# Twenty more split tiles of q and k, token numbers written once a batch, interleaved last products, five accumulators for x, and weights ahead of counts, in a kernel of attention over channels and a mixture of experts

## The chip, the cores and the metric

The kernel runs on one core of a Trainium2 chip. The time is that of the device, in microseconds (us), for one launch; of several runs the median counts. The engines are TensorE (PE in the profile, PEld its weight loads), VectorE (DVE), ScalarE (ACT), GpSimd (POOL) and SyncE (SP, which here only issues DMAs).

## The reference

```python
# q, k, v: (B=4, N=3648, C=256)
qn = q / (norm(q, axis=1) + 1e-6); kn = k / (norm(k, axis=1) + 1e-6)
s = kn.transpose(0, 2, 1) @ qn / tau          # (B, C, C): over channels
a = softmax(s, -1)
x = (v @ a).reshape(14592, 256)
# 16 experts: 4 groups of 4; each token goes to the best group's best expert
g_w = softmax(x @ w_group)[best group]
e_w = softmax(x @ w_expert[group])[best expert]
out[token] = g_w * e_w * (relu(x @ w1[g, e]) @ w2[g, e])      # 256 -> 1024 -> 256
```

All is fp32. Both softmaxes of the routing add 1e-9 to their sum.

## The kernel before

**Attention.** A batch has 3648 rows, that is 28 tiles of 128 and a rest of 64. They are read in units of 4 tiles (q and k together, 512 rows, tile `qkraw`); a batch has 8 units, the eighth is the rest. Unit `u` belongs to batch `u // 8`. `s_load` reads a unit, `s_split` prepares it, `s_mm` adds its products k^T q to the accumulator `sacc` in PSUM, `s_add` sums the squares for the norms. An fp32 product shows as two records on PE, so a plain tile is 4 records (two halves of k). In all units but the rests and two others the tile `SPLIT = 3` goes another way: ACT copies it rounded to fp32r (`qkhi`, L195), DVE subtracts that from the original (`qklo`, L196), and three fp32r products, hi·hi, hi·lo and lo·hi, take the place of the fp32 one: 6 records per tile. There are 26 such tiles. After a batch's last unit, `softmax` makes the matrix `a`, split into `ahi` and `alo` too (L292), with 20 routing columns beside the 256.

**x and the routing.** `x_tr` transposes v on PE (`vtr`), and splits it into `vth` (ACT, L313) and `vtl` (DVE, L314). `x_mm` makes each row tile of x and its 20 logits by six fp32r products of 276 columns into one of three PSUM accumulators (`xmm`, tag `mm`); ACT empties it into `xs` (L335), a ring of 10 tiles of 4 rows each. The 20 logits are copied to `L`, by DVE (L342), or by ACT (L340) when `x_mm` is called with hooks, as in the last batch. The generator `routing(b, j0, j1)` (L349 to L425) works on a range of row tiles, in nine calls (`RANGES`): first the one-hot of the best expert, its running count (`inc`, L387), then the slot numbers `si` (bs at L400 to si at L409), then the weights (sw at L412 to the reciprocal at L423, which goes straight into column 257 of `xs`). `scatter` (L430 to L455) sends one row tile to its slots in DRAM (`x_sorted`): POOL writes the token numbers into column 256 of `xs` (an iota per group of four tiles, L441, or L443 for the rest), issues the indirect DMA (L444), and fills a tile with zeros (L158) as a pause. SP fetches the first item's rows (L676) when batch 2's tiles below 20 have been scattered.

**Experts.** 28 items of 512 sorted rows: transposes (L747), first layer (L898), second layer (L918 wide, hi part; L919 narrow, low part), weighting and a send per 128 rows (indirect DMA on POOL, L947). The last item ends with four turns (L1233 to L1243): wide products (L1238) into the accumulator of 128 rows, ACT reads its one half with the weight (L1239), narrow products (L1241) into the other half, DVE adds it (L1242), send.

The order of SP and POOL is written by hand throughout. PE, ACT and DVE are ordered by a scheduler up to the 30th step of a loop over units, and by hand from there (`hooks`, lists of small steps between the row tiles of x).

Of the kernel before, what the change touches and what calls it, by code (L numbers as in the profile page):

```python
# [17 lines left out]
P = 128  # L18
# [6 lines left out]
NJ = J + 1  # L25
# [27 lines left out]
PLAIN = (GPB + 1, GPB + 2)  # L53
US = UX = B * GPB
XOFF = GPB + 2
VX = 1
# [4 lines left out]
def attention_moe(ctx: ExitStack, tc, q, k, v, tau, w_group, w_expert, w1, w2, out):  # L61
# [89 lines left out]
    for n in range(4):  # L151
        DVE.memset(lane4[n * PC:(n + 1) * PC, n:n + 1], 1.0)
    zero = cp.tile([P, RW], F32, name="zero")
# [32 lines left out]
    def s_split(u):  # L186
        b, g = divmod(u, GPB)
        rows, nj = rows_of(g)
        x, d = su[u], st[b]
        raw = x["raw"]  # L190
        x["split"] = SPLIT if g < NG and u not in PLAIN else None
        if x["split"] is not None:
            x["hi"] = spool.tile([P, 2, C], F32R, tag="hi", name="qkhi")
            x["lo"] = spool.tile([P, 2, C], F32R, tag="lo", name="qklo")
            ACT.activation(x["hi"], raw[:, :, SPLIT, :], AF.Copy)  # L195
            DVE.tensor_tensor(x["lo"], raw[:, :, SPLIT, :], x["hi"], ALU.subtract)  # L196
        if g == 0:
# [15 lines left out]
    def s_mm(u):  # L213
        b, g = divmod(u, GPB)
        rows, nj = rows_of(g)
        x, d = su[u], st[b]
        for j in range(nj):
            if j == x["split"]:
                hi, lo = x["hi"], x["lo"]
# [97 lines left out]
    def x_mm(u, hooks=None):  # L317
# [9 lines left out]
        for j in range(nj):  # L327
            mm = ps.tile([P, 512], F32, tag="mm", name="xmm", bufs=3)
# [10 lines left out]
        if hooks:  # L339
            ACT.activation(Lx, xs[:rows, :nj, C:NE], AF.Copy)  # L340
        else:
            DVE.tensor_copy(Lx, xs[:rows, :nj, C:NE])  # L342


    scatters, pend, now, rows_at, early = [], [], [0], {}, []
# [4 lines left out]
    def routing(b, j0=0, j1=NJ):  # L350
# [31 lines left out]
        if j1 == NJ:  # L382
            DVE.memset(oh[REM:, :, nj - 1:nj], 0.0)
        yield
# [7 lines left out]
        ez = wide("ez", NL)  # L392
        ACT.activation(ez, z, AF.Exp)
        pp = pt.tile([P, 512], F32, tag="misc", name="pp", bufs=1)
        with tc.high_priority(offset=0 if now[0] >= TM else -1040):
            PE.matmul(pp[:, 0:E], tri, rs, start=True, stop=False, skip_group_check=True)
            PE.matmul(pp[:, E:2 * E], onesb, rs, start=False, stop=True, skip_group_check=True)
        yield
# [11 lines left out]

        sw = wide("sw", 5).rearrange("p (j g) -> p j g", g=5)
        DVE.tensor_reduce(sw, ez.rearrange("p (j g e) -> p j g e", g=5, e=4), AX.X, ALU.add)  # L412
        yield
        sg = wide("sg", 4).rearrange("p (j g) -> p j g", g=4)
        DVE.tensor_tensor(sg, sw[:, :, 1:5], ohg, ALU.mult)
        se = wide("se", 1)
        DVE.tensor_reduce(se, sg, AX.X, ALU.add)
        DVE.tensor_scalar(se, se, 1e-9, None, ALU.add)
        DVE.scalar_tensor_tensor(se, sw[:, :, 0], 1e-9, se, ALU.add, ALU.mult)

        for g in range(j0 // GJ, -(-j1 // GJ)):
            n = min(GJ, j1 - g * GJ)
            DVE.reciprocal(rows_at[b, g][:, 0:n, C + 1], se[:, g * GJ - j0:g * GJ - j0 + n])  # L423
# [6 lines left out]
    def scatter(n, wait=0):  # L430
        for _ in range(n):
# [22 lines left out]
            pause()  # L454

# [718 lines left out]
    for n in range(len(seq) + lag):  # L1174
# [56 lines left out]
        if n == len(seq) + lag - 1:  # L1231
# [3 lines left out]
            for t in (0, 2, 1, 3):  # L1235
                tsl, a, wcol = slice(t * P, (t + 1) * P), d["acc"][t], d["wc"][:, t:t + 1]
                for f in range(8 - TAIL, 8):
                    PE.matmul(a, d["h", f][0][:, tsl], d["w2w"][:, :, f, :], start=False, stop=(f == 7), skip_group_check=True)  # L1238
                ACT.activation(d["ys"][:, t, :], a[:, 1, :], AF.Copy, scale=wcol)  # L1239
                for f in range(8 - TAIL, 8):  # L1240
                    PE.matmul(a[:, 0, :], d["h", f][1][:, tsl], d["w2h"][:, f, :], start=False, stop=(f == 7), skip_group_check=True)  # L1241
                DVE.scalar_tensor_tensor(d["ys"][:, t, :], a[:, 0, :], wcol, d["ys"][:, t, :], ALU.mult, ALU.add)  # L1242
# [94 lines left out]
```

## Time and profile before

| | us |
|---|---|
| median of 3 runs (lowest, highest) | 931.75 (929.29, 934.0) |
| profiled execution, its own time | 935.83 |
| profiled execution, span | 934.1 |
| PE, busy in the span | 916.0 |
| DVE, busy | 707.0 |
| ACT, busy | 481.4 |
| POOL, busy | 403.1 |

The span runs from the first instruction to the last. Busy times of different engines overlap. The chain that ended last follows the work back from the end, at each step to what released it. A line such as "L196 DVE" is an instruction's line in the kernel; "out<-in" are its tiles, and "xcount" how many instructions stand in the row.

### The profile page before, as it was taken

How to read it: one execution, taken by the hardware profiler on the slowest of the kernel's cores; microseconds unless marked ns; L12 is line 12 of the kernel's file. 1: busy time of each engine (PE TensorE's matmuls, PEld its weight loads, DVE VectorE, ACT ScalarE, POOL GpSimd, SP SyncE). 2: the span in 40 equal slices, each digit the busy share in tenths (PEclk: the TensorE clock that was granted, in tenths of full speed). 3: DMA queues.
4: the chain of work that ended last, by engine and by line, in shares of the span. 5: the costliest groups of instructions: out<-in, count | busy, mean ns of one | idle time of the engine just before them, and what ended most of it. 6: DMA issues, size and time to landing. Idle time of an engine off the chain costs nothing.

```text
span 934.1 us, 17126 instructions
## 1 busy us (share of the span) xinstructions
PE 916.0 (98%) x5620; PEld 771.7 (83%) x5620; DVE 707.0 (76%) x1478; ACT 481.4 (52%) x791; POOL 403.1 (43%) x573
## 2 busy tenths in 40 slices
PE   9999999998999999999999999999999999999996
PEld 7898998987899988888888887888888888888884
DVE  6888968766889877978775778678766877687742
ACT  6787677556654544444444444444444444444431
POOL 0001888986578682223222433343334333333222
PEclk9999999999999999999999999999999999999999
DMA  9974868355855577677777777777777767776740
GB/s 305 350 284 174 302 230 278 143 192 183 265 175 175 201 231 240 226 241 256 243 242 245 254 251 244 243 248 239 228 237 232 248 226 228 234 242 231 235 136 27
DMA packets 159172, 213.97 MB, mean 229 GB/s; under 512 B 63107, under 2 KB 117643, under 8 KB 159072
## 3 DMA queue, kind: packets, MB, share of 16 engines
q1 hardware_dynamic: 144128, 168.23, 55.2%
q0 software_dynamic: 14944, 44.54, 12.6%
q8 instruction: 46, 0.75, 0.3%
q14 instruction: 54, 0.44, 0.1%
HBM read 170.33 MB, written 31.39 MB: 216 GB/s over the span
## 4 chain that ended last, share of the span: by engine, by line
PE 73%; issue 9%; DMA 5%; POOL 5%; DVE 4%; ACT 3%; SPq 1%; POOLq 0%; ACTq 0%; DVEq 0%
PE hmm L898 28%; PE wacc L918 16%; PE wacc L919 8%; PE xmm L332 6%; PE yacc L927 5%; PE sacc L227 4%; DMA qkraw<-in_k 3%; POOL out L947 2%; PE qacc L1034 2%; PE qmm L1021 2%; PE vtr L312 2%; DVE sqa L211 2%; POOL x_sorted L444 1%; POOL zero L158 1%; DMA xg<-x_sorted,ix_big 1%
## 5 line engine op out<-in xcount | busy, mean ns | idle before, releaser
L898 PE MATMUL hmm<-xth,ww 128*128 128x512 f32 x896 | 316.1, 394 | 0.1
L907 ACT ACTIVATE hh<-hmm 128x512 fp32r<-128x512 f32 x222 | 133.6, 602 | 346.7 <-PE hmm L898 316.1
L947 POOL DMA_INDIRECT out<-ys,ids x112 | 133.8, 1195 | 385.0 <-DVE ys L936 355.4
L918 PE MATMUL wacc<-ww,hh 128*128 128x512 f32 x752 | 274.7, 398 | 0.0
L908 DVE SCALAR_TENSOR_TENSOR hl<-hmm,hh 128x512 fp32r<-128x512 f32 x222 | 153.0, 690 | 133.8 <-ACT hh L907 118.9
L919 PE MATMUL wacc<-ww,hl 128*128 128x256 f32 x752 | 210.8, 280 | 0.0
L898 PEld LDWEIGHTS hmm<-xth,ww 128*128 128x128 f32 x896 | 168.1, 188 | 38.1 <-ACT xth L748 0.4
L898 PE MATMUL hmm<-xtl,ww 128*128 128x512 f32 x448 | 177.3, 396 | 0.2 <-DVE xtl L749 0.2
L918 PEld LDWEIGHTS wacc<-ww,hh 128*128 128x128 f32 x752 | 141.3, 188 | 43.2 <-issue 7.8
L444 POOL DMA_INDIRECT x_sorted<-xs,si x112 | 133.5, 1192 | 65.0 <-issue 31.9
L919 PEld LDWEIGHTS wacc<-ww,hl 128*128 128x128 f32 x752 | 141.1, 188 | 6.9
L709 DVE TENSOR_TENSOR ww<-wraw,ww 128x1024 fp32r<-128x1024 f32 x112 | 136.8, 1221 | 13.1 <-ACT ww L708 12.0
L708 ACT ACTIVATE ww<-wraw 128x1024 fp32r<-128x1024 f32 x112 | 118.6, 1059 | 0.0
L898 PEld LDWEIGHTS hmm<-xtl,ww 128*128 128x128 f32 x448 | 84.5, 189 | 10.5 <-DVE xtl L749 0.5
L227 PE MATMUL sacc<-qkraw 128*128 128x256 f32 (+1 forms) x360 | 87.0, 385 | 1.2 <-DMA qkraw<-in_k 1.2
L158 POOL MEMSET zero<- 128x256 f32 x264 | 87.8, 333 | 0.3
L332 PE MATMUL xmm<-ahi,vth 128*128 128x276 f32 (+1 forms) x232 | 70.2, 305 | 4.9 <-ACT xs L335 3.8
L227 PEld LDWEIGHTS sacc<-qkraw 128*128 128x128 f32 (+1 forms) x360 | 65.5, 192 | 10.1 <-issue 2.2
L332 PE MATMUL xmm<-alo,vth 128*128 128x276 f32 (+1 forms) x232 | 67.6, 292 | 0.2 <-DVE alo L292 0.2
L332 PE MATMUL xmm<-ahi,vtl 128*128 128x276 f32 (+1 forms) x232 | 66.9, 289 | 0.0
L211 DVE TENSOR_TENSOR sqa<-sqa,sq 128x2048 f32<-128x2048 f32 (+1 forms) x28 | 57.6, 2056 | 10.4 <-ACT sq L203 10.0
L335 ACT ACTIVATE xs<-xmm 128x276 f32<-128x276 f32 x112 | 42.6, 405 | 37.3 <-PE xmm L332 23.2
(269 smaller groups left out, 1283.2 us busy)
## 6 DMA issues: line engine op xcount, KB each, us to landing
wraw<-in_moe_w SPq DMA_DIRECT2D x55, 1024.0 KB
wraw<-in_moe_w SPq DMA_DIRECT2D x50, 512.0 KB
qw<-in_moe_w SPq DMA_DIRECT2D x48, 512.0 KB
vr<-in_v SPq DMA_DIRECT2D x28, 512.0 KB
qkraw<-in_q SPq DMA_DIRECT2D x26, 512.0 KB
qkraw<-in_k SPq DMA_DIRECT2D x26, 512.0 KB
xq<-xg SPq DMA_DIRECT2D x368, 32.0 KB
x_sorted<-xs,si POOLq DMA_INDIRECT x112
```

What stands on the lines that cost most here:

```text
L158: POOL.memset(zero[:, 0:256], 0.0)
L227: PE.matmul(d["acc"][:, c, :], kt[:rows, 1, cs], qt[:rows, 0, :], start=d.pop("first", True) and c == 0, stop=(g == NG), skip_group_check= ...
L332: PE.matmul(mm[:rows, :NE], vt[:, c, j * P:j * P + rows], at[:, c, :], start=(n == 0), stop=(n == 5))
L444: ins = POOL.indirect_dma_start(out=xs_d, out_offset=bass.IndirectOffsetOnAxis(ap=si[:rows, j:j + 1], axis=0), in_=xs[:rows, t, 0:RW].bitc ...
L708: ACT.activation(whs[n][:, s], raw[:, s], AF.Copy)
L709: DVE.tensor_tensor(wls[n][:, s], raw[:, s], whs[n][:, s], ALU.subtract)
L898: PE.matmul(mm, wt[:, c, fs], xt[:, c, :], start=(n == 0), stop=(n == 5))
L907: ACT.activation(hh, mm, AF.Relu)
L908: d["hl"] = DVE.scalar_tensor_tensor(hl, mm, 0.0, hh, ALU.max, ALU.subtract)
L918: PE.matmul(d["acc"][t], hh[:, tsl], d["w2w"][:, :, f, :], start=(f == 0), stop=(f == 7), skip_group_check=True)
L919: PE.matmul(d["acc"][t][:, 0, :], hl[:, tsl], d["w2h"][:, f, :], start=False, stop=(f == 7), skip_group_check=True)
L947: ins = POOL.indirect_dma_start(out=out, out_offset=bass.IndirectOffsetOnAxis(ap=d["ids"][:, t:t + 1], axis=0), in_=d["ys"][:, t, :], in_o ...
```

## The change

1. `MORE` names 20 further tiles to be split: tile 2 in units 14 to 27 (12 of them, since the rests are left out), tiles 1 and 2 of unit 28, tiles 0, 1 and 2 of units 29 and 30. Their hi and lo parts use buffers `hh` and `hl`, which are the experts' later (3 of each).
2. The token numbers go to a tile `tok`, by two iotas for a batch (all 28 tiles, and the rest), those of the first two batches at the start, the others behind a batch's last scatter. The reciprocal goes to `tok` as well, once per routing call, and small DVE instructions (an OR with 0) copy number and weight into `xs`, one for each group of tiles.
3. The last products: wide 0, wide 2, narrow 0, wide 1, narrow 2, wide 3, narrow 1, narrow 3, with a send behind each narrow.
4. In the last batch two of five row tiles of x take an `acc` buffer as accumulator, beside the three `mm`.
5. In `routing` the exponential comes one step earlier, and weights and copies to `xs` stand ahead of the slot numbers; one step fewer.
6. The copy to `L` is always ACT's.

```diff
+MORE = {**{u: (2,) for u in range(GPB + 6, 28)}, 28: (1, 2), 29: (0, 1, 2), 30: (0, 1, 2)}
+NTOK = 2
...
+    tok = cp.tile([P, NTOK, NJ, 2], F32, name="tok")
+    def number(b):
+        o = tok[:, b % NTOK, :, 0].bitcast(I32)
+        POOL.iota(o[:, 0:J], pattern=[[-1, J]], base=NOID - b * NT, channel_multiplier=-J)
+        POOL.iota(o[:, J:NJ], pattern=[[0, 1]], base=NOID - b * NT - J * P, channel_multiplier=-1)
+    for b in range(NTOK):
+        number(b)
...
-        x["split"] = SPLIT if g < NG and u not in PLAIN else None
-        if x["split"] is not None:
-            x["hi"] = spool.tile([P, 2, C], F32R, tag="hi", name="qkhi")
-            x["lo"] = spool.tile([P, 2, C], F32R, tag="lo", name="qklo")
-            ACT.activation(x["hi"], raw[:, :, SPLIT, :], AF.Copy)
-            DVE.tensor_tensor(x["lo"], raw[:, :, SPLIT, :], x["hi"], ALU.subtract)
+        x["split"] = {}
+        for j in (*MORE.get(u, ()), SPLIT) if g < NG and u not in PLAIN else ():
+            if j == SPLIT:
+                hi, lo = [spool.tile([P, 2, C], F32R, tag=n, name="qk" + n) for n in ("hi", "lo")]
+            else:
+                hi, lo = [hp.tile([P, 512], F32R, tag=n, name=n).rearrange("p (i c) -> p i c", i=2) for n in ("hh", "hl")]
+            ACT.activation(hi, raw[:, :, j, :], AF.Copy)
+            DVE.tensor_tensor(lo, raw[:, :, j, :], hi, ALU.subtract)
+            x["split"][j] = hi, lo
...
-            mm = ps.tile([P, 512], F32, tag="mm", name="xmm", bufs=3)
+            spread.append(u)
+            if hooks and d is st[B - 1] and len(spread) % 5 < 2:
+                mm = ps.tile([P, 2, C], F32, tag="acc", name="xmm").rearrange("p c n -> p (c n)")
+            else:
+                mm = ps.tile([P, 512], F32, tag="mm", name="xmm", bufs=3)
...
-        if hooks:
-            ACT.activation(Lx, xs[:rows, :nj, C:NE], AF.Copy)
-        else:
-            DVE.tensor_copy(Lx, xs[:rows, :nj, C:NE])
+        ACT.activation(Lx, xs[:rows, :nj, C:NE], AF.Copy)
...
+        DVE.reciprocal(tok[:, b % NTOK, j0:j1, 1], se)
+        for g in range(j0 // GJ, -(-j1 // GJ)):
+            n = min(GJ, j1 - g * GJ)
+            DVE.tensor_single_scalar(rows_at[b, g][:, 0:n, C:C + 2].bitcast(I32),
+                                     tok[:, b % NTOK, g * GJ:g * GJ + n, :].bitcast(I32), 0, op=ALU.bitwise_or)
...
-        for g in range(j0 // GJ, -(-j1 // GJ)):
-            n = min(GJ, j1 - g * GJ)
-            DVE.reciprocal(rows_at[b, g][:, 0:n, C + 1], se[:, g * GJ - j0:g * GJ - j0 + n])
...
-            if t == 0:
-                tok = xs[:, 0:nj, C].bitcast(I32)
-                if g < NG:
-                    POOL.iota(tok, pattern=[[-1, GJ]], base=NOID - b * NT - g * GJ, channel_multiplier=-J)
-                else:
-                    POOL.iota(tok, pattern=[[0, 1]], base=NOID - b * NT - J * P, channel_multiplier=-1)
...
+            if j0 + j == NJ - 1 and b + NTOK < B:
+                number(b + NTOK)
...
+            turns = (0, 2, 1, 3)
+            wide_of(turns[0])
+            for t, nxt in zip(turns, (*turns[1:], None)):
+                if nxt is not None:
+                    wide_of(nxt)
+                narrow_of(t)
                 send(d, t)
```

The order of instructions shows three places. On PE, the last products of the last item, before the change; `wacc` with its number is the accumulator of 128 rows, `eh` and `hh` are hi parts of the hidden layer, `el` and `hl` low parts:

```order
L1238 MATMUL wacc_12239<-ww3_3702,eh_12297 128x512 x2
L1238 MATMUL wacc_12239<-ww3_3702,hh_12333 128x512
L1238 MATMUL wacc_12239<-ww3_3702,hh_12344 128x512
L1241 MATMUL wacc_12239<-ww3_3702,el_12298 128x256 x2
L1241 MATMUL wacc_12239<-ww3_3702,hl_12334 128x256
L1241 MATMUL wacc_12239<-ww3_3702,hl_12345 128x256
L1238 MATMUL wacc_12241<-ww3_3702,eh_12297 128x512 x2
```

And the same place after it, where the lines are L1248 (wide) and L1254 (narrow):

```order
L1248 MATMUL wacc_12385<-ww3_3879,eh_12443 128x512 x2
L1248 MATMUL wacc_12385<-ww3_3879,hh_12479 128x512
L1248 MATMUL wacc_12385<-ww3_3879,hh_12490 128x512
L1248 MATMUL wacc_12387<-ww3_3879,eh_12443 128x512 x2
L1248 MATMUL wacc_12387<-ww3_3879,hh_12479 128x512
L1248 MATMUL wacc_12387<-ww3_3879,hh_12490 128x512
L1254 MATMUL wacc_12385<-ww3_3879,el_12444 128x256 x2
L1254 MATMUL wacc_12385<-ww3_3879,hl_12480 128x256
L1254 MATMUL wacc_12385<-ww3_3879,hl_12491 128x256
L1248 MATMUL wacc_12386<-ww3_3879,eh_12443 128x512 x2
```

Between the wide and the narrow products of one accumulator now stand the wide ones of the next. On DVE, the routing call for tiles 8 to 20 of batch 2, before the change (`vtl` belongs to x, `inc` to `si` are the slot numbers, `sw` to the reciprocal the weights):

```order
L390 CAST rs<-inc 128x16
L288 COPY ax<-awp 128x2x20
L292 TENSOR_TENSOR alo<-ax,ahi 128x552
L314 TENSOR_TENSOR vtl<-vtr,vth 128x512 x2
L400 TENSOR_TENSOR bs<-pp,carry 128x16
...
L409 CAST si<-sf 128x12
L412 TENSOR_REDUCE sw<-ez 128x60
...
L423 RECIPROCAL xs<-se 128x4 x3
L314 TENSOR_TENSOR vtl<-vtr,vth 128x512 x2
```

And after it:

```order
L407 CAST rs<-inc 128x16
L302 COPY ax<-awp 128x2x20
L306 TENSOR_TENSOR alo<-ax,ahi 128x552
L328 TENSOR_TENSOR vtl<-vtr,vth 128x512 x2
L414 TENSOR_REDUCE m_2819<-ez 128x60
...
L421 RECIPROCAL tok<-se 128x12
L424 TENSOR_SCALAR xs<-tok 128x4x2 x3
L428 TENSOR_TENSOR bs<-pp,carry 128x16
...
L437 CAST si<-sf 128x12
```

The weights moved ahead of the slot numbers, and one reciprocal with three copies stands for three reciprocals. On POOL, the scatters of one group and the next before the change:

```order
L444 DMA x_sorted<-xs,si 238080x272
L158 MEMSET zero 128x256
L441 IOTA xs 128x4
L444 DMA x_sorted<-xs,si 238080x272
L158 MEMSET zero 128x256
```

And after it, at the end of a batch:

```order
L452 DMA x_sorted<-xst,si 238080x272
L169 MEMSET zero 128x256
L159 IOTA tok 128x28
L160 IOTA tok 128x1
L452 DMA x_sorted<-xs,si 238080x272
```

An iota stands no longer ahead of each group of four scatters; two stand behind a batch's last one (and four at the start of the program).

## Rows read from the trace of the kernel before

**Rows 1.** The page: busy time by engine, and the chain that ended last.

```profile
PE 916.0 (98%) x5620; PEld 771.7 (83%) x5620; DVE 707.0 (76%) x1478; ACT 481.4 (52%) x791; POOL 403.1 (43%) x573
...
PE 73%; issue 9%; DMA 5%; POOL 5%; DVE 4%; ACT 3%; SPq 1%; POOLq 0%; ACTq 0%; DVEq 0%
```

**Rows 2.** Windows: length, busy time of each engine (instructions), granted clock, DMA share, GB/s.

```profile
100.00:140.00 40.00, 39.58 (x274) 36.92 (x274) 32.54 (x76) 27.24 (x48) 35.95 (x48) 1.00 0.77 270
140.00:180.00 40.00, 39.46 (x271) 36.49 (x271) 35.60 (x86) 28.02 (x52) 34.60 (x47) 1.00 0.68 232
180.00:196.00 16.00, 16.00 (x108) 14.72 (x106) 9.33 (x26) 7.35 (x14) 14.11 (x25) 1.00 0.29 96
...
232.00:236.00 4.00, 3.63 (x30) 3.41 (x29) 3.11 (x8) 3.43 (x10) 0.00 (x0) 1.00 0.60 176
```

**Rows 3.** PE's timeline around 106 us: start, length, instruction, [idle before].

```profile
105.63 1.89 PE L227 MATMUL sacc<-qkraw 128*128 128x256 f32 x8
...
107.48 0.28 PE L227 MATMUL sacc<-qklo,qkhi 128*128 128x256 f32 x1
...
107.95 0.28 PE L227 MATMUL sacc<-qkhi,qklo 128*128 128x256 f32 x1
108.07 0.96 PE L285 MATMUL awp<-wcat,aT 128*128 128x20 f32 x8
```

**Rows 4.** The tile qkhi: ns shortest/median/longest, first and last start; who waited.

```profile
L227 PE MATMUL sacc<-qklo,qkhi x52: 278/282/387, 8.5 to 191.8; 128*128 128x256 f32 x52
...
L196 DVE TENSOR_TENSOR qklo<-qkraw,qkhi x26: 672/684/694, 7.8 to 178.6; 128x512 fp32r<-128x512 f32 x26
...
  PEld sacc L227: 0.6, 2
```

**Rows 5.** The same view, from 140 to 180 us alone.

```profile
L195 ACT ACTIVATE qkhi<-qkraw x5: 616/630/645, 149.4 to 177.1; 128x512 fp32r<-128x512 f32 x5
```

**Rows 6.** Line L342, DVE's copies of the logits.

```profile
L342 DVE COPY L<-xs x18: 170/195/424, 62.1 to 188.3; 128x80 f32<-128x80 f32 x18
```

**Rows 7.** PE's waits, 196 to 246 us: who for whom, total, times, longest.

```profile
PE xmm L332 <- ACT xs L335: 3.3, 6, 1.3
PE xmm L332 <- ACT vth L313: 0.8, 1, 0.8
```

**Rows 8.** PE's timeline in the last turns.

```profile
922.69 0.50 PE L1241 MATMUL wacc<-ww,el 128*128 128x256 f32 x2 [0.56 <-ACT ys L1239]
```

**Rows 9.** POOL's timeline, 900 us to the end: sends.

```profile
903.25 0.97 POOL L947 DMA_INDIRECT out<-ys,ids  x1 [16.10 <-DVE ys L936]
...
904.71 0.98 POOL L947 DMA_INDIRECT out<-ys,ids  x1 [0.17 <-issue]
...
922.06 0.97 POOL L947 DMA_INDIRECT out<-ys,ids  x1 [9.63 <-DVE ys L1242]
...
928.77 0.97 POOL L947 DMA_INDIRECT out<-ys,ids  x1 [0.93 <-DVE ys L1242]
```

**Rows 10.** Line L441, the iotas.

```profile
L441 POOL IOTA xs<- x28: 137/151/165, 62.3 to 298.5; 128x4 int32 x28
```

**Rows 11.** POOL's timeline, scatters at 108, 120 and 212 us.

```profile
108.20 2.50 POOL L444 DMA_INDIRECT x_sorted<-xs,si  x1 [0.16 <-issue]
...
120.69 0.98 POOL L444 DMA_INDIRECT x_sorted<-xs,si  x1 [0.28 <-POOL xs L441]
...
212.82 0.98 POOL L444 DMA_INDIRECT x_sorted<-xs,si  x1 [2.81 <-issue]
```

**Rows 12.** SP's timeline: the first fetch of sorted rows.

```profile
232.11 0.35 SPq L676 DMA_DIRECT2D wraw<-x_sorted  x1
```

**Rows 13.** PE's timeline: the first transposes of sorted rows.

```profile
241.42 1.11 PE L747 MATMUL xtr<-ident,wraw 128*128 128x128 f32 x8
```

**Rows 14.** DVE's timeline around the first two scatters of rows 11.

```profile
107.58 2.28 DVE L211 TENSOR_TENSOR sqa<-sqa,sq 128x2048 f32<-128x2048 f32 x1
...
120.89 0.68 DVE L196 TENSOR_TENSOR qklo<-qkraw,qkhi 128x512 fp32r<-128x512 f32 x1
```

More of the change, by code (lines that the diff above doesn't have):

```diff
@@ L217, in s_mm @@
         for j in range(nj):
-            if j == x["split"]:
-                hi, lo = x["hi"], x["lo"]
+            if j in x["split"]:
+                hi, lo = x["split"][j]
                 terms = (hi, hi), (hi, lo), (lo, hi)
@@ L338, in x_mm @@
         Lx = d["L"][:rows, g * GJ:g * GJ + nj, :]
-        if hooks:
-            ACT.activation(Lx, xs[:rows, :nj, C:NE], AF.Copy)
-        else:
-            DVE.tensor_copy(Lx, xs[:rows, :nj, C:NE])
-    scatters, pend, now, rows_at, early = [], [], [0], {}, []
+        ACT.activation(Lx, xs[:rows, :nj, C:NE], AF.Copy)
+    scatters, pend, now, rows_at, early, spread = [], [], [0], {}, [], []
     def bc(x, n):
@@ L383, in routing @@
             DVE.memset(oh[REM:, :, nj - 1:nj], 0.0)
+        ez = wide("ez", NL)
+        ACT.activation(ez, z, AF.Exp)
         yield
@@ L391, in routing @@
         yield
-        ez = wide("ez", NL)
-        ACT.activation(ez, z, AF.Exp)
         pp = pt.tile([P, 512], F32, tag="misc", name="pp", bufs=1)
@@ L397, in routing @@
             PE.matmul(pp[:, E:2 * E], onesb, rs, start=False, stop=True, skip_group_check=True)
+        sw = wide("m5", 5).rearrange("p (j g) -> p j g", g=5)
+        DVE.tensor_reduce(sw, ez.rearrange("p (j g e) -> p j g e", g=5, e=4), AX.X, ALU.add)
+        sg = wide("sg", 4, "scr0").rearrange("p (j g) -> p j g", g=4)
+        DVE.tensor_tensor(sg, sw[:, :, 1:5], ohg, ALU.mult)
+        se = wide("se", 1)
+        DVE.tensor_reduce(se, sg, AX.X, ALU.add)
+        DVE.tensor_scalar(se, se, 1e-9, None, ALU.add)
+        DVE.scalar_tensor_tensor(se, sw[:, :, 0], 1e-9, se, ALU.add, ALU.mult)
+        DVE.reciprocal(tok[:, b % NTOK, j0:j1, 1], se)
[3 more added lines that the diff above has]
+                                     tok[:, b % NTOK, g * GJ:g * GJ + n, :].bitcast(I32), 0, op=ALU.bitwise_or)
         yield
@@ L409, in routing @@
         DVE.tensor_copy(si, sf)
[L411 to L419, printed above, removed]
-        for g in range(j0 // GJ, -(-j1 // GJ)):
-            n = min(GJ, j1 - g * GJ)
-            DVE.reciprocal(rows_at[b, g][:, 0:n, C + 1], se[:, g * GJ - j0:g * GJ - j0 + n])
         pend.extend(((b, j0), now[0], j, si) for j in range(nj))
@@ L1234, in attention_moe, with wide_of, narrow_of @@
             d["ys"] = ring(4, C, name="ys")
-            for t in (0, 2, 1, 3):
-                tsl, a, wcol = slice(t * P, (t + 1) * P), d["acc"][t], d["wc"][:, t:t + 1]
+            def wide_of(t):
+                a = d["acc"][t]
                 for f in range(8 - TAIL, 8):
-                    PE.matmul(a, d["h", f][0][:, tsl], d["w2w"][:, :, f, :], start=False, stop=(f == 7), skip_group_check=True)
-                ACT.activation(d["ys"][:, t, :], a[:, 1, :], AF.Copy, scale=wcol)
+                    PE.matmul(a, d["h", f][0][:, t * P:(t + 1) * P], d["w2w"][:, :, f, :], start=False, stop=(f == 7), skip_group_check=True)
+                ACT.activation(d["ys"][:, t, :], a[:, 1, :], AF.Copy, scale=d["wc"][:, t:t + 1])
+            def narrow_of(t):
+                a = d["acc"][t]
                 for f in range(8 - TAIL, 8):
-                    PE.matmul(a[:, 0, :], d["h", f][1][:, tsl], d["w2h"][:, f, :], start=False, stop=(f == 7), skip_group_check=True)
-                DVE.scalar_tensor_tensor(d["ys"][:, t, :], a[:, 0, :], wcol, d["ys"][:, t, :], ALU.mult, ALU.add)
+                    PE.matmul(a[:, 0, :], d["h", f][1][:, t * P:(t + 1) * P], d["w2h"][:, f, :], start=False, stop=(f == 7), skip_group_check=True)
+                DVE.scalar_tensor_tensor(d["ys"][:, t, :], a[:, 0, :], d["wc"][:, t:t + 1], d["ys"][:, t, :], ALU.mult, ALU.add)
+            turns = (0, 2, 1, 3)
[4 more added lines that the diff above has]
+                narrow_of(t)
                 send(d, t)
```

## Prediction

> **What bounds the kernel now.** I read the page first. TensorE (PE) is busy for 98% of the span and the chain that ended last lies on it for 73% [rows 1]: whatever shortens PE's own work, or closes one of its few gaps, comes off the end; work of the others costs only where it makes PE late. So the views that matter are those of PE: the windows, to see in which stage PE is full and who has room beside it, then PE's timeline for the price of a product, then its waits. From 100 to 180 us PE is busy 79.04 of 80 us at a granted clock of 1.00, and VectorE (DVE) has 7.46 us free in the first half and 4.40 in the second [rows 2]. All changed parts lie before 245 us or after 918 us; between these the order of work is the same, and I cost it at nothing.
>
> The sum is made against the profiled execution, 935.83 us, which is 4.1 above the median of the runs, 931.75; I carry the difference over to the median.
>
> **Twenty more split tiles.** Eight records of plain q and k products (two tiles) and six of a split tile take 2.44 us from 105.63 to 108.07 [rows 3]. The fp32r products of the split tile start 0.118 apart (four steps from 107.48 to 107.95), so the six take 0.71 and the eight 1.73, 0.216 each. A plain tile is 4 x 0.216 = 0.864, a split one 0.71: 0.154 gained per tile, 20 x 0.154 = 3.1 us, in a stretch in which PE is the bound. For that ScalarE (ACT) makes 20 copies of 0.630 = 12.6 us [rows 5], and DVE 20 subtractions of 0.684 = 13.7 us [rows 4]. Are they hidden? The units that get more than one are the last: of the twenty, ten belong to the five units whose copies start between 140 and 180 us [rows 5], which is 6.8 us of DVE against 4.4 free. DVE gives away 18 copies of L of 0.195 us [rows 6], 3.5 us in all between 62 and 188 us, so some 1.1 in these 40 (an estimate by proportion), and about 1.3 us slides beyond 180, where 6.7 of 16 us are free [rows 2]. The cover there is the lead of the splits: the last subtraction starts at 178.6, the last product that reads one at 191.8 [rows 4]. Behind a late subtraction stand, on DVE, the sums of squares and the low parts of v, and PE's transposes wait for those. With 26 such tiles PE waited 0.6 us for them [rows 4]; 20 more in proportion cost 0.5. I take **-2.6**, with ends of 0 and -3.1. ACT has 12 us free in each 40 [rows 2]; with 20 copies and the L copies it stays below 90%, and I cost it at nothing.
>
> **Five accumulators for x in the last batch.** From 196 to 246 us PE's products for x wait six times, 3.3 us, for ACT to empty an accumulator, at most 1.3 at once [rows 7]. A row tile is six products of 276 columns, 6 x 0.118 x 276/256 = 0.76 us, so two more accumulators let PE run 1.5 us further ahead: more than the longest wait. I take **-3.3**. The ends: 0, if PE instead stops at the next operand (high and low parts of v), and 4.9: where PE waits 0.56 in the tail, a turn of 2.24 us has only 1.41 of products (next part), so a wait shown as 0.56 can cost 0.83, and 3.3 + 6 x 0.27 = 4.9 [rows 8].
>
> **The last products.** Now each narrow product stands behind its own wide one and ACT's reading of it: 0.56 us idle in each turn [rows 8], and a turn is 2.24 us (three from 922.06 to 928.77 [rows 9]). The products of one turn are four of 512 columns (0.235 each, two steps of 256) and four of 256: 0.94 + 0.47 = 1.41. With the next wide product between, PE has something to do while ACT reads, and a turn would be 1.41. The first send does not move: the first narrow waits for wide 2 (0.94 us) instead of for ACT, which is about the same as the gap. But the sends go through GpSimd (POOL): 1.46 us from one to the next when nothing is missing, as at 903.25 and 904.71 [rows 9]. So POOL sets the pace: sends at 922.06 + 3 x 1.47 = 926.5 in place of 928.77. **-2.3**, ends -2.0 and -2.5 (PE's own 3 x 0.83).
>
> **Token numbers, weights ahead of counts.** POOL has 8 iotas instead of 32; one is 0.151 us [rows 10]. Ahead of the first item's rows 21 go and 4 come: 17 x 0.151 = 2.6 us less in front of the scatters, if a larger one takes as long as a small one. DVE swaps 32 reciprocals for 9, and gets 32 small copies: equal. But the scatter of tile 8 of batch 2, the first of a routing call, stood idle for 2.81 us until DVE had the call's counts and weights [rows 11]. In the new order the same DVE instructions, counts last, still stand ahead of it: it comes no earlier, and only POOL's slack before it grows, from 2.8 to 5.4. The weights reach xs earlier and wait for no iota. After that scatter two iotas are gone, 0.3 us. The first gather of rows is issued at 232.11 [rows 12], its transposes come at 241.42 [rows 13]. It is 0.56 MB; at 176 GB/s [rows 2] it has landed by 236, 5.4 us ahead. PE arrives 5.9 earlier (2.6 + 3.3), and the routing that releases the scatters moves with PE by most of 2.6: near, not binding. I take **0**, with +2.9 (below) and 0 as ends.
>
> The sum: 2.6 + 3.3 + 2.3 = 8.2 us: 935.83 - 8.2 = 927.6 for the profiled one, **923.5** against the median.
>
> **A rule that speaks against it.** Rows first: a scatter that began 0.62 us after a DVE sum of two SBUF operands took 2.50 us instead of 0.98 (108.20 [rows 11], 107.58 [rows 14]); another, begun 0.20 before a subtraction of the same kind, took 0.98, and the subtraction kept its 0.68 (120.69 [rows 11], 120.89 [rows 14]). So it is the order that decides, and each new subtraction can hold a scatter for up to its 0.684 us: 20 x 0.684 = 13.7 on POOL at most, minus 2.6 of iotas and 2.8 of slack: the gather 8.3 later, landing at 244.3 instead of 236, 2.9 after its present use. Then all that PE gained before is lost and the end is 931.75 + 2.9 - 2.3 = 932.3, the far end of rival C. The Trainium skill ("SBUF — State Buffer", section "Who interferes with whom") says that a VectorE instruction with two SBUF inputs contends with a GpSimd one that reads SBUF, and that whoever issues first keeps the other out for the whole instruction. By that rule my 0 for POOL would be up to these 8 us; the first pair of rows agrees, the second shows a subtraction that was not kept out though it came second. POOL is busy about 1 us of 1.47 with scatters, so most subtractions begin inside one; I expect a small part, some 3 us, which the slack takes.
>
> **The rivals.**
> A, the forecast: 923.5. Chance 0.61.
> B, the accumulators bring nothing: PE's waits in the x stage move to ACT's and DVE's parts of v, which are made at the same pace. For it: ACT gets the L copies of other batches too, and DVE late subtractions. Against: of the waits there, 3.3 us are for ACT's emptying and 0.8 for v's high part [rows 7]. 931.75 - 2.6 - 2.3 = 926.9. Chance 0.16.
> C, POOL is held, so that the first gather lands when it is used today: PE's gains before the experts go, the tail stays: 931.75 - 2.3 = 929.5. It bites from 5 us of holding (2.6 and 2.8 taken off) and takes all at 11, of the 13.7 possible. Chance 0.11.
> D, slower: DVE becomes the bound between 140 and 192 us. If none of the 20 subtractions is hidden, 13.7 us stand against 3.1 + 3.3 + 2.3 = 8.7: 931.75 + 5.0 = 936.7. It turns to a loss from 13 of the 20 exposed. For it: 6.8 us of work in 4.4 us of room. Against: 0.6 us of waits for 26, and a lead of 13 us. Chance 0.07.
> E, no change: waits go elsewhere and the tail is set by the last transfers to land: 931.5. Chance 0.05.
>
> **How the numbers follow.** About 0.5%, 4.7 us, can be told from no change: below 927.1 is faster, above 936.4 slower. A is faster but for its poorest ends, B half: 0.61 x 0.94 + 0.16 x 0.6 = 0.67. D is slower, with some room for a mishap of C: 0.07. The rest, 0.26, is the same. The range takes in A, B and C: down to the best ends, 931.75 - 3.1 - 4.9 - 2.5 = 921.2, and up to C's 929.5; the three runs of before lie up to 2.5 us from their median, so I add 1.5 below and 0.5 above: 919.7 to 930.0.
>
> **What would show it.** Right: 4 records of 0.216 replaced by 6 of 0.118 in twenty more tiles, and no more than 1 us of PE waits for the new low parts; PE's waits for ACT's emptying between 196 and 246 us near zero; the transposes of the first item 5 to 6 us earlier, with no wait of PE for the gather; sends in the tail 1.47 us apart. Wrong: PE waits of several us for low parts or for v's parts in the same stretch (D, B); scatters of 1.5 us and more in large numbers, and a PE wait for the first item's rows (C); sends still over 2 us apart.

## The result, and the profile after

The changed kernel took **942.27 us** (median of 4 runs, 941.68 to 942.82); the kernel before took 931.21 on the same chip (4 runs, 929.29 to 934.0). The ratio is 1.0121, 95% interval 1.0102 to 1.0141: slower by 11 us where 8 less were forecast. The profiled execution took 942.0 us, with a span of 940.3. It lies 6.2 us above that of before (935.83), not 11, because before's profiled execution was itself over 4 us above its medians (931.21 and 931.75); what follows compares these two traces. Of all executions behind the times of this document one was slow, 1117.65 us, of after in set 4, and the ratios leave it out.

The page of after. PE is no less the bound than in [rows 1]: 2.5 us more busy, and its idle time has grown too, from 934.1 - 916.0 = 18.1 to 940.3 - 918.5 = 21.8 us.

```profile
PE 918.5 (98%) x5660; PEld 775.7 (82%) x5660; DVE 716.8 (76%) x1487; ACT 494.1 (53%) x831; POOL 397.0 (42%) x549
...
PE 69%; issue 7%; DMA 7%; DVE 6%; ACT 4%; POOL 3%; SPq 3%; POOLq 0%; another core or an unknown queue 0%; ACTq 0%; DVEq 0%
```

Where is it lost? The same instruction of PE, found in both traces, is 4.0 us earlier after the change at 191 us and 6.0 earlier at 223: so far the forecast holds. At 248 us the lead is gone, at 280 after is 6.2 us behind. From there to 914 us it falls back by another 2.4 us: 0.7 up to 342 us, the rest evenly. In the last turns it regains 2.4. So there are two losses: one between 223 and 280 us, one spread over the experts.

PE's waits in after, 196 to 300 us (who for whom, total, times, longest). ACT's emptying of x, 3.3 us in [rows 7], is gone from the list; four others stand there.

```profile
PE pp L411 <- DVE rs L407: 3.9, 2, 2.3
PE yacc L937 <- ACT ys L948: 3.0, 2, 2.6
PE vtr L326 <- issue: 1.6, 1, 1.6
PE vtr L326 <- DVE vtl L328: 1.2, 1, 1.2
```

The new one is `pp`. These are the two small products with which a routing call counts tokens over partitions; their input `rs` is the call's last running count, cast by DVE. In PE's timeline of after (start, length, instruction, [idle before]) two of them hold PE up:

```profile
223.84 2.00 PE L326 MATMUL vtr<-ident,vr 128*128 128x128 f32 x8 [1.59 <-issue]
...
229.55 0.17 PE L411 MATMUL pp<-rs,tri 128*128 128x16 bf16 x1 [1.58 <-DVE rs L407]
...
238.65 1.11 PE L757 MATMUL xtr<-ident,wraw 128*128 128x128 f32 x8
...
246.45 0.17 PE L411 MATMUL pp<-rs,tri 128*128 128x16 bf16 x1 [2.34 <-DVE rs L407]
...
276.01 0.50 PE L937 MATMUL yacc<-ww,hh 128*128 128x256 f32 x2 [2.58 <-ACT ys L948]
```

The same two calls in the kernel before, PE's timeline and then DVE's: the cast of `rs` starts at 234.47 and 251.76, 1.74 and 0.90 us before `pp` starts, and no idle time stands in the rows.

```profile
236.21 0.18 PE L396 MATMUL pp<-rs,tri 128*128 128x16 bf16 x1
...
252.66 0.18 PE L396 MATMUL pp<-rs,tri 128*128 128x16 bf16 x1
```

```profile
234.47 0.18 DVE L390 CAST rs<-inc 128x16 bf16<-128x16 f32 x1
...
251.76 0.44 DVE L390 CAST rs<-inc 128x16 bf16<-128x16 f32 x1
```

In after DVE casts them at

```profile
229.32 0.17 DVE L407 CAST rs<-inc 128x16 bf16<-128x16 f32 x1
...
246.19 0.21 DVE L407 CAST rs<-inc 128x16 bf16<-128x16 f32 x1
```

DVE is earlier by 5.2 and 5.6 us, but PE reaches `pp` earlier still: it would have been there at 229.55 - 1.58 = 227.97 and 244.11, 8.2 and 8.6 us earlier than before. In the order of the two programs `pp` stands behind 109 row tiles of x before and behind 105 after, and the next behind 4 and 2 groups of first-layer products: four row tiles (4 x 0.76 us) and two groups closer to the front. That is what "one step fewer" in `routing` does. The calls run as small steps between the row tiles, one call after the other, so a call that ends a step earlier moves all later ones ahead, on PE as on DVE.

Behind the waits the clock falls. Windows of before, then of after: length, PE, PEld, DVE, ACT, POOL busy, granted clock, DMA share, GB/s.

```profile
212.00:232.00 20.00, 16.83 (x128) 15.71 (x127) 12.07 (x45) 10.95 (x28) 15.90 (x27) 1.00 0.48 171
232.00:250.00 18.00, 17.32 (x116) 15.22 (x115) 15.39 (x41) 13.00 (x32) 7.97 (x12) 1.00 0.72 229
250.00:300.00 50.00, 50.00 (x327) 45.36 (x327) 45.56 (x125) 24.32 (x40) 41.45 (x66) 1.00 0.59 202
```

```profile
212.00:232.00 20.00, 16.30 (x116) 15.21 (x114) 10.78 (x39) 9.65 (x25) 11.78 (x19) 0.91 0.46 152
232.00:250.00 18.00, 15.38 (x95) 13.47 (x93) 16.04 (x43) 10.92 (x26) 12.27 (x17) 0.93 0.77 260
250.00:300.00 50.00, 46.97 (x290) 41.90 (x289) 42.11 (x109) 20.61 (x32) 38.55 (x58) 0.96 0.57 189
```

There are three stretches of 3.41 us at the lower level (0.5, which is 1.2 GHz), from 223.63, 247.52 and 278.24. Each begins between 0.2 us before and 2.3 us after the end of an idle time of PE of 1.6 to 2.6 us; the idle time that ends at 229.55, 1.58 us, has none. Eight transposes take 2.00 us at 223.84, where the eight at 231.21 take 1.04. By the windows the three cost 0.09 x 20 + 0.07 x 18 + 0.04 x 50 = 5.1 us. That is why PE's busy time grew although its work shrank.

The second loss shows between two instructions that every version has. PE's timeline of before, then of after: the first product `qmm`, and the first product of the last turns.

```profile
342.45 0.41 PE L1021 MATMUL qmm<-wraw,qxT 128*32 128x256 f32 x2
...
918.54 0.63 PE L1238 MATMUL wacc<-ww,eh 128*128 128x512 f32 x2
```

```profile
349.30 0.41 PE L1031 MATMUL qmm<-wraw,qxT 128*32 128x256 f32 x2
...
927.16 0.62 PE L1248 MATMUL wacc<-ww,eh 128*128 128x512 f32 x2
```

576.09 us before, 577.86 after, with no idle time of PE and no lower clock in it. I call this the middle; what lies ahead of it is the head, up to `qmm`, and what lies behind, to the end of the span, the tail: 15.56 us before, 13.14 after.

### The profile page after: what moved, and what is told of

Read it like the earlier page. It is cut to its first block, busy times and chain, and to the rows that moved or that the text cites. A ratio compares the mean times of both kernels' runs of the same rounds, so it can differ in the third digit from the quotient of the medians.

```text
span 940.3 us, 17270 instructions
## 1 busy us (share of the span) xinstructions
PE 918.5 (98%) x5660; PEld 775.7 (82%) x5660; DVE 716.8 (76%) x1487; ACT 494.1 (53%) x831; POOL 397.0 (42%) x549
## 4 chain that ended last, share of the span: by engine, by line
PE 69%; issue 7%; DMA 7%; DVE 6%; ACT 4%; POOL 3%; SPq 3%; POOLq 0%; another core or an unknown queue 0%; ACTq 0%; DVEq 0%
PE hmm L908 25%; PE wacc L928 13%; PE wacc L929 7%; PE sacc L241 6%; PE xmm L350 6%; PE yacc L937 5%; DMA qw<-in_moe_w 3%; POOL out L957 2%; PE qmm L1031 2%; PE vtr L326 2%; SPq L696 2%; PE qacc L1044 2%; DMA xq<-xg 1%; DVE sqa L225 1%; DVE vtl L328 1%
## 5 line engine op out<-in xcount | busy, mean ns | idle before, releaser
L241 PE MATMUL sacc<-qkraw 128*128 128x256 f32 (+1 forms) x280 | 67.9, 384 | 1.2 <-DMA qkraw<-in_k 1.2
L1016 DVE STREAM_TRANSPOSE qhT<-qh 32x128 f32<-32x128 f32 x192 | 57.6, 300 | 2.7
```

## The experiments

Five sets ran, the first being the result above. Sets two to five ran on chips 12, 0, 2 and 0; which chip the result ran on isn't on record. Each ratio is against the kernel before in the same set, and times of different sets aren't subtracted. Head, middle and tail are those of the one profiled execution of each kernel. Rows that don't begin with "before" are the changed kernel with the edits named.

| kernel | median us (before) | ratio, 95% | head | middle | tail |
|---|---|---|---|---|---|
| result: after | 942.27 (931.21) | 1.0102 to 1.0141 | 349.30 | 577.86 | 13.14 |
| set 2: step | 935.12 (930.10) | 1.0032 to 1.0077 | 339.19 | 577.85 | 14.76 |
| iotas back | 937.18 | 1.0047 to 1.0091 | 345.73 | 577.86 | 13.21 |
| step, iotas back | 933.94 | 1.0022 to 1.0056 | 341.39 | 577.95 | 13.16 |
| before + last products | 928.34 | 0.9962 to 1.0000 | 335.60 | 576.08 | 12.82 |
| set 3: step, pad | 924.64 (928.53) | 0.9947 to 0.9973 | 333.45 | 576.61 | 13.04 |
| step, pad, three accumulators | 925.29 | 0.9952 to 0.9979 | 333.91 | 576.61 | 13.18 |
| before + last products + splits | 925.97 | 0.9968 to 0.9988 | 334.00 | 576.60 | 12.90 |
| before + last products + accumulators | 926.10 | 0.9958 to 0.9981 | 334.52 | 576.08 | 14.20 |
| set 4: after | 931.96 (928.18) | 1.0023 to 1.0043 | 338.69 | 577.85 | 14.66 |
| after, step | 926.41 | 0.9972 to 0.9990 | 333.45 | 577.86 | 13.39 |
| after, pad | 930.14 | 1.0011 to 1.0033 | 338.49 | 576.90 | 13.01 |
| after, step, pad | 925.26 | 0.9950 to 0.9976 | 333.33 | 576.61 | 13.26 |
| set 5: after | 931.68 (928.15) | 1.0030 to 1.0056 | 337.40 | 577.86 | 13.14 |
| step, pad | 925.28 | 0.9962 to 0.9985 | 333.37 | 576.61 | 13.12 |
| step, pad, hh and hl as before | **924.65** | 0.9952 to 0.9977 | 333.44 | 576.08 | 13.28 |
| the last without the splits | 929.20 | 1.0000 to 1.0018 | 338.74 | 576.08 | 13.08 |

**Set 2: the step, the iotas, the last products alone.** The step is one line at the end of `routing`; with it `pp` stands behind 109 row tiles and 4 and 10 groups again, as before.

```diff
         pend.extend(((b, j0), now[0], j, si) for j in range(nj))
         yield
+        yield
```

> The changed kernel with one more empty step at the end of each routing call, so that the count products pp stand on PE where they stood before (behind 109 row tiles of x and behind 4 and 10 groups of the first layer, instead of 105, 2 and 8). Nothing else differs. Theory S (the step taken out moved pp ahead of DVE's rs, and PE waits in order): the waits of pp for rs, 1.58 and 2.34 us, go, and with them the two stretches of lower clock that follow them, some 1.7 us each: 7 us less than the changed kernel, about 935. Theory T (POOL's unbroken train of scatters, without the iotas, holds up PE's signals): pp is a by-product, 1 to 2 us less, about 941.

The second puts the 32 iotas back into `scatter`, in front of each group's first scatter, which slows POOL and leaves PE's order as it is.

> The changed kernel with the 32 iotas back in front of the groups of scatters (they write the same numbers again), so that POOL's train is broken every four scatters as before. Theory T: ACT gets PE's signals in time, the wait of yacc for ACT's ys near 274 us (3.0 us and a stretch of lower clock, 1.7) goes, and part of the stop near 222 us: 5 us less than the changed kernel, about 937. Theory S: the waits of pp stay as they are, and POOL's later scatters cost nothing or something: 942 to 943.

> Both edits of the two runs beside it. If both theories hold, 7 and 5 us less: about 930. If S alone holds, as the run with the step, about 935; if T alone, as the run with the iotas, about 937. If neither, 942: then the cause lies in the splits or the five accumulators.

The fourth is the kernel before with the last products interleaved, and nothing else.

> The kernel before with the interleaved last products alone. By the sum of the prediction 2.3 us less than before (2.0 to 2.5), about 928.9: POOL's sends 1.47 us apart. If the transfers at the end set the time, no difference.

With the step the kernel is at 1.0055, without it and with the iotas at 1.0069; this chip has larger spreads than sets three to five, and the two intervals overlap. After itself didn't run in this set, so the times by which theories S and T were to be told apart (935, 937, 941) can't be judged here. The traces say more: with the step the two waits of `pp` are gone, with the iotas alone `pp` waits 3.75 and 2.34 us. Theory T's sign, that ACT gets PE's signals in time with the iotas back, failed: between 196 and 246 us 14 of ACT's 35 readings of an accumulator of x still start over 1 us after the end of its last product (18 of 36 in after). Step and iotas together show the mechanism of rival C, in PE's waits from 120 to 300 us: POOL is later, the gather is issued at 233.79, and PE stands for its rows.

```profile
PE xtr L764 <- DMA wraw<-x_sorted: 5.0, 1, 5.0
```

Without the iotas there is no such wait, so the 2.6 us taken from POOL matter once PE is early. The last products alone bring 0.9981, and their trace holds a surprise for another term. PE's waits from 196 to 246 us:

```profile
PE xmm L332 <- ACT xs L335: 0.7, 1, 0.7
```

Up to 918 us that is the kernel before, with its three accumulators; where its profiled execution waited 3.3 us [rows 7], this one waited 0.7. In the former 22 of ACT's 41 readings between 196 and 246 us start over 1 us after the end of the accumulator's last product, in the latter 3 of 38.

**Set 3: which parts bring something.** `tok` and the smaller tiles of `routing` shift the pools behind them by 96 bytes in SBUF; 96 bytes of padding put them back, all but `hh` and `hl`, which stay 224 bytes lower, since the new splits ask for them ahead of three small tiles of the same pool.

```diff
     tok = cp.tile([P, NTOK, NJ, 2], F32, name="tok")
+    DVE.memset(cp.tile([P, 24], F32, name="pad"), 0.0)
```

> The changed kernel with the extra step, and 96 bytes of padding beside tok, so that the pools behind (v and its parts, the items' rows xth and xtl, three of the four weight buffers) lie at the SBUF addresses of the kernel before instead of 96 bytes lower; the hidden layer's hh and hl lie 224 lower instead of 320. Theory P (where these tiles lie sets the pitch of the products: the trace has 237.9 ns instead of 235.9 between a wide product on hh and the one on hl, and 2.5 to 3 us are lost evenly from 300 to 900 us in all kernels with tok): the loss goes or changes, 932.5 against 935.1 with the step alone. Rival (the loss comes from other work beside PE): 935.

> As the run beside it, with three accumulators for x as before. The prediction's term for the accumulators says 3.3 us slower. Theory G (with two more PE only runs further ahead of ACT and then stands longer in one piece, and the first gather is the bound anyway): the same, or up to 2 us faster, where a stretch of lower clock goes.

> The kernel before with the interleaved last products and the twenty more split tiles, nothing else. By the prediction's term 2.6 us less than with the last products alone (928.3): 925.7. Theory G (the gather of the first item, which starts when the scatters are done, holds PE): less than 1 us of it arrives, 927.5 or more; the transposes of the first item would show a wait for the gather.

> The kernel before with the interleaved last products and five accumulators for x. By the prediction's term 3.3 us less than 928.3: 925. Theory G: the same as 928.3 within 1 us, since the profiled run of before had longer waits there than most runs (the run with the last products alone shows 0.7 us).

Step and pad turn the loss into a gain, 0.9960. The times expected for the first two theories (932.5 and 935) were those of another chip and can't be judged; the middle, 576.61 us against 577.85 with the step alone in set 2, goes with theory P. With three accumulators in place of five it is 0.65 us more, within the intervals: so little is left of the 3.3 us, as theory G expected.

The last products alone didn't run in this set, so the other two are compared with each other. The accumulators differ only behind 192 us; up to there this pair shows the splits alone. PE's timelines, the last products of q and k, with the splits and then with the accumulators:

```profile
189.30 1.13 PE L231 MATMUL sacc<-qkraw 64*128 64x256 f32 x4
```

```profile
190.54 1.13 PE L227 MATMUL sacc<-qkraw 64*128 64x256 f32 x4
```

The splits lead by 1.24 us there, of which 0.41 stand already at 55 us, ahead of their first product (the 30th row tile of x starts at 54.83 and 55.24). So they bring 0.8, not 2.6: between 60 us and this place PE stands idle for 2.15 us with them and for 1.00 without. At `qmm` the lead is 0.52 (334.00 to 334.52), the middle loses as much (576.60 to 576.08), and the medians are equal within their intervals (925.97 and 926.10).

**Set 4: step and pad, each alone, on one chip.** After unchanged, with the step, with the pad, with both.

> The changed kernel itself once more, beside the three others on one chip, since the runs so far were on different chips: 1.012 of the kernel before if the loss belongs to the kernel; 1.006 to 1.008 if a part of it belonged to the chip of its first runs (there and in the runs with the extra step, PE's signals to ACT came up to 6 us after the end of the products, while scatters ran; in the runs with the padding, on another chip, none came late).

> The changed kernel with the extra step (run before on another chip at 1.0055). Theory S: 0.7% below the changed kernel on this chip too. Theory P (the 96 bytes): stays over 1.003. If the chip made the difference between 1.0055 and 0.996, it comes to 0.998 or less here where before shows no late signals.

> The changed kernel with 96 bytes of padding and without the extra step. Theory P: 2.5 to 9 us less than the changed kernel on this chip, the drift from 300 to 900 us goes from 2.5 us to under 1. Theory S: the waits of pp for rs and the stretches of lower clock stay, so that it is 5 to 7 us above the run with both edits.

> Both edits again (0.996 on another chip). If steps and padding are separate causes, it stands below each of the two single edits by the other's effect; 0.996 again if it doesn't hang on the chip.

This is the set that settles the main cause: 931.96, 926.41, 930.14 and 925.26. The step takes 5.55 us, and 4.88 where the pad is there; the pad 1.82, and 1.15 where the step is. PE's waits from 196 to 300 us in after,

```profile
PE pp L411 <- DVE rs L407: 3.1, 2, 2.3
PE vtr L326 <- DVE vtl L328: 1.6, 1, 1.6
```

and with the step:

```profile
PE vtr L326 <- DVE vtl L328: 0.5, 1, 0.5
```

3.1 + 1.1 us of waits and one stretch at the lower level (granted clock 0.94 from 232 to 260 us, 0.06 x 28 = 1.7 us) make 5.9, for 5.2 in the heads and 5.55 measured. In none of this set's traces does ACT read an accumulator late: between 196 and 246 us at most one reading in each, by 1.0 us. So the step's 5.55 us don't hang on that. And after lost 3.8 us here, not 11: less than either case of the expectation.

**Set 5: what was still open.** Three small tiles asked for ahead of the first split put `hh` and `hl` at their old addresses; the last kernel is that with step and pad and `MORE = {}`, where they lie there by themselves.

```diff
+    DVE.memset(hp.tile([P, 4], I32, tag="ids", name="ids", bufs=4), 0)
+    DVE.memset(hp.tile([P, 4], F32, name="wc", bufs=1), 0.0)
+    DVE.memset(hp.tile([P, 4], I32, tag="keep4", name="keep", bufs=2), 0)
```

> The changed kernel once more, to stand beside the three variants on one chip. Theory (the count products come ahead of their input in TensorE's queue, product pitch, no more) expects about 932 of 928 (1.003 to 1.004), two waits of TensorE for rs of 3 to 4 us in sum. Rival (signals to ACT and TensorE that arrive late while POOL scatters, seen on two chips out of four) expects 935 to 942 and a wait of yacc for ACT's ys of over 2 us near 275 us, on a chip on which before's own trace shows ACT reading accumulators over 1 us after their last product.

> One more step at routing's end and 96 bytes beside the token numbers. Theory expects 0.996 of before (-3.5 us). Rival (the gain on another chip was chance) expects 0.998 to 1.000.

> The kernel with step and pad, in which three small tiles of the pool of hh and hl are asked for ahead of the first split, so that hh and hl lie at before's addresses again. Theory (addresses of a product's operands set its pitch) expects 1 us less than the kernel with step and pad alone (0.995 of before), and a wide product on hh every 235.9 ns as in before. Rival (the pitch comes from what other engines read then) expects the same time and 236.5 ns.

> The kernel with step and pad, without the twenty splits; hh and hl lie at before's addresses then. If a split's saved time is kept to the end, it takes 2 to 3 us more than the kernel with hh and hl at before's addresses; if the gather and the order of the stage of x set where that stage ends, less than 1 us more.

The middle, from PE's timelines: step and pad, then with `hh` and `hl` as before.

```profile
333.37 0.41 PE L1033 MATMUL qmm<-wraw,qxT 128*32 128x256 f32 x2
...
909.98 0.40 PE L1250 MATMUL wacc<-ww,eh 128*128 128x512 f32 x1
```

```profile
333.44 0.41 PE L1036 MATMUL qmm<-wraw,qxT 128*32 128x256 f32 x2
...
909.52 0.63 PE L1253 MATMUL wacc<-ww,eh 128*128 128x512 f32 x2
```

576.61 and 576.08: the latter is before's middle to 0.01 us. The middles of the table fall into groups: 576.1 with every pool of the experts where it was, 576.6 with `hh` and `hl` moved, 577.9 with the 96 bytes; the pad without the step, 576.9, lies beside the second and has an idle time of 0.10 us in it. From the start of a wide product on `hh` to that of the next on `hl` (mean of 752) it is 236.1 ns before, 238.0 in after, 236.5 with step and pad and 236.3 in the last kernel but one: there the middle came back in full, but this step only by half, so my 235.9 for it was off. Other steps move too: between two products on `xth` of the first layer lie 230.7, 234.0, 230.9 and 230.8 ns. The medians, 925.28 and 924.65, differ by less than their intervals.

Without the splits the kernel is 4.55 us slower, more than either case of the expectation and than any sum of products explains. Its trace has a wait that the other has not (PE's waits, 120 to 300 us; then ACT's timeline, then the window from 160 to 180 us):

```profile
PE xmm L351 <- ACT ahi L306: 2.3, 1, 2.3
```

```profile
161.43 1.91 ACT L218 ACTIVATE sq<-qkraw 128x2048 f32<-128x2048 f32 x1 [4.16 <-DMA qkraw<-in_k]
```

```profile
160.00:180.00 20.00, 17.72 (x114) 16.40 (x113) 14.51 (x39) 10.41 (x22) 18.18 (x24) 0.91 0.53 183
```

ACT waits 4.16 us for a unit of q and k, the sums of squares and the attention matrix come late, PE waits 2.3 us for `ahi` and then runs at the lower level (0.09 x 20 = 1.8 us). That is 4.1 of the 5.30 by which its head is longer; 1.2 are left for the splits' own products. That the unit lands late has to do with PE itself: SP issues its transfer when PE's products on an earlier unit have freed the buffer (SP's waits for `sacc` are 38.2 us between 120 and 165 us), and that is 2.27 us later without the splits. SP's timelines, without and with them:

```profile
153.86 0.33 SPq L195 DMA_DIRECT2D qkraw<-in_q  x1
```

```profile
151.59 0.33 SPq L198 DMA_DIRECT2D qkraw<-in_q  x1
```

The rest of the lateness wasn't tried.

## Why the prediction was wrong

**The step that failed** is the paragraph on token numbers and weights with its "I take **0**". I costed the new order of `routing` on DVE ("the same DVE instructions, counts last") and on POOL, and never looked at PE, where the two `pp` of each call stand in order among the row tiles of x. The change moved them ahead by about 3 us against DVE, with margins of 1.74 and 0.90 us that stood in the trace of before. I had named PE as the engine on which any closed gap comes off the end; the same holds for a gap that opens. Undone by one line, it gives back 5.55 us (set 4), and with that the kernel there is faster than before (0.9972 to 0.9990); on the chip of set 2 it is still slower (1.0032 to 1.0077). **A second step failed** with "between these the order of work is the same, and I cost it at nothing": the order is the same, and yet the middle takes 1.77 us more.

**Splits, 2.6 us.** The price per product was right: in after's timeline hi and lo products of split tiles start 0.118 apart, and DVE's 15 new subtractions into `hl` took 0.682 each between 100 and 190 us. At 191 us after led by 4.0 us over the profiled before, but the kernel with the last products alone, which has before's order up to 918 us, led by 1.4 there too. In set 3 the splits are worth 0.8 us at that place, 0.1 at `qmm` and nothing that shows in the whole time; in set 5 1.2 may be their own, and 4 more came because they keep another wait away. So the term was mis-sized: waits of PE took over 1 us of the gain against the 0.5 that I allowed, and the rest must be kept through the routing, the x stage and the shift of `hh` and `hl`.

**Five accumulators, 3.3 us.** Mis-sized: at most 0.7 (0.65 in set 3). The 3.3 us were waits of one profiled execution, which lay 4.1 us above the median and in which ACT read many accumulators late; another one of the same stage waited 0.7. I took them off the profiled execution and then carried the sum to the median, though nothing showed that a median execution has them. Rival B was right on the amount, but its cause is shown only in part: PE's waits for v's low parts are 1.2 us in after and 1.6 in set 4, where before has none, but most of the 3.3 us were hardly there to move.

**Last products, 2.3 us.** Right: the tail shrinks from 15.56 to 13.14 us in the traces, 2.4 (12.8 to 14.8 in the table), and POOL's sends in after run at its own pace. POOL's timeline:

```profile
930.80 0.97 POOL L957 DMA_INDIRECT out<-ys,ids  x1 [9.89 <-DVE ys L1255]
932.26 0.97 POOL L957 DMA_INDIRECT out<-ys,ids  x1 [0.17 <-issue]
```

Alone it measured 930.10 - 928.34 = 1.8.

**Token numbers, 0.** For POOL right. The gather is issued 3.2 us earlier (228.94 against [rows 12]) and the transposes start at 238.65, 2.8 earlier than [rows 13], where I had 5 to 6, and without a wait. For PE wrong, as said above. For SBUF wrong too: of the 1.8 us in the middle the 96 bytes that `tok` and the smaller tiles shift cost 1.0 to 1.3 (577.85 to 576.90 and 577.86 to 576.61), and the early place of `hh` and `hl`, which the splits bring, the other 0.5.

**The rule on shared SBUF access** had little to do with it: scatters of over 1.3 us between 98 and 236 us are 12 in after and 11 before, with 20 more subtractions. One took 6.14 us (at 111.25), longer than any before. With the splits alone, in set 3, they are 18 against 11, but what they take beyond 0.98 us sums to 15 and 16 us. The Trainium skill ("SBUF — State Buffer", section "Who interferes with whom") would allow one such hold for each subtraction; the trace shows that it didn't add up here.

**The rivals.** A, the forecast, failed by sign, and E, no change, by the prediction's own bound of 936.4. C's mechanism exists, but it showed only with step and iotas together. D gave the right sign for another reason: no wait of PE for a split's low part stands in after's lists. The time fell outside the range because no case had a wait on the routing's path.

**Which part stays open.** The same program lost 11 us in the result and 3.8 and 3.5 in sets 4 and 5. From 196 to 300 us the waits for `pp` are of like size in the three traces (3.9, 3.1 and 3.1 us), but that of the result adds 3.0 us for `ys` and has three stretches at the lower level there, against one and none. The last section shows what goes with it; its cause wasn't found. So the change is slower in all three sets, and the two reasons shown account for the loss in sets 4 and 5; what came on top in the result stays open.

The lowest times measured are those of after with step and pad, with `hh` and `hl` at their old addresses (924.65 us, 0.9964 of before) or not (924.64 in set 3, 0.9960): the two are not told apart.

## What to carry to other kernels

When a generator of small steps gets a step shorter, list on every in-order engine what moves ahead, and compare each move with the margin between its input and its start in the trace: here 3 us against 1.74 and 0.90 from start to start. Size a term from a wait only if more than one profiled execution shows it, or if the profiled one lies near the median. After adding a tile, compare the pitch of untouched products in the long stretch as well.

## What the runs showed of the hardware that I had not expected

**A few hundred bytes in SBUF set the pitch of products.** PE is full in the middle in all versions, with the clock at 1.00, the same products and the same order, and yet 1.9 ns in 236 between wide and narrow, and 3.3 in 231 between two hi products of the first layer, come and go with the addresses; the middle takes 576.08 to 577.95 us accordingly. Why an address does that no run shows.

**An idle time of about 2 us on PE can cost nearly twice its length.** From 20 to 330 us PE has, in all traces together, seven idle times of 2.2 to 2.6 us, and around the end of six of them (0.4 us before it to 2.3 behind) a stretch of 3.41 us at a granted clock of 0.5 begins, which costs 1.7. The seventh is in set 5's run of after: `pp` waited 2.34 us as well and the clock stayed at 1.00. Of six idle times of 1.5 to 1.8 us only one has such a stretch, that which ends at 223.84 in after.

**Signals that seem to arrive late, in some executions.** In the result's trace of after, half of ACT's readings of an accumulator of x between 196 and 246 us start more than 1 us after the end of PE's last product for it, up to 6.1. ACT's and POOL's timelines of three in a row:

```profile
217.43 0.40 ACT L353 ACTIVATE xs<-xmm 128x276 f32<-128x276 f32 x1 [0.87 <-DMA x_sorted<-xs,si]
218.91 0.40 ACT L353 ACTIVATE xs<-xmm 128x276 f32<-128x276 f32 x1 [1.08 <-PE xmm L350]
220.43 0.40 ACT L353 ACTIVATE xs<-xmm 128x276 f32<-128x276 f32 x1 [1.12 <-PE xmm L350]
```

```profile
216.62 0.97 POOL L452 DMA_INDIRECT x_sorted<-xs,si  x1 [0.16 <-issue]
218.11 0.97 POOL L452 DMA_INDIRECT x_sorted<-xs,si  x1 [0.17 <-issue]
219.57 0.97 POOL L452 DMA_INDIRECT x_sorted<-xs,si  x1 [0.16 <-issue]
```

Each of the three starts 0.80 to 0.86 us after a scatter does, though PE fills an accumulator every 0.76 us. Over all 18 late ones that distance goes from 0.2 to 2.4 us, so it isn't shown that the scatters set them. In set 5 the same kernel's readings keep PE's pace, with scatters as dense:

```profile
216.35 0.40 ACT L353 ACTIVATE xs<-xmm 128x276 f32<-128x276 f32 x1 [0.37 <-PE xmm L350]
217.12 0.40 ACT L353 ACTIVATE xs<-xmm 128x276 f32<-128x276 f32 x1 [0.36 <-PE xmm L350]
```

Before's trace of the first set shows such late readings too, 22 of 41, in the stretch of [rows 7]. In set 2 the three kernels with `tok` have 14 to 17 of them and that with the last products alone 3; in the traces of sets 3 to 5 no kernel has more than one. So it isn't a matter of the program alone: the same one has 18 in the result and none in sets 4 and 5. Whether the chip, the occasion or the execution decides is not shown.
